# First keys through GpSimd in bf16, first queries through SyncE in fp32, and another order of the same work in an attention and mixer kernel

## The chip, the cores and the metric

The kernel runs on one core of one Trainium2 chip. The metric is the device time of one execution in microseconds; 352.54 us before, the median of three runs from 350.51 to 353.13. Every time below is in microseconds from the start of the profiled span if nothing else is said.

## The reference

Eight batches, twelve heads, sequence 448, head width 64. Attention with a squared ReLU in place of a softmax gives x (8 x 448 x 768); a token mixing and a channel mixing with two matrices each follow:

```
scores = (1/8) * q @ k.T
x      = (max(scores, 0)**2 / 448) @ v          # heads side by side: 768 columns
u      = x + (max(x.T @ w_tok1, 0) @ w_tok2).T  # 448 -> 256 -> 448
out    = u + max(u @ w_ch1, 0) @ w_ch2          # 768 -> 1536 -> 768
```

## The kernel before

**Tiling.** Four heads of one batch make a set; the 8 batches give 24 sets, numbered s. A set's keys, queries and values lie on 128 partitions in seven pieces c of 64 positions. `load` (L287) brings them in by GpSimd's queue, which turns fp32 into bf16 on the way: `ldk{s}`, `ldq{s}`, `ldv{s}`. For the sets 0 and 1 keys and queries come in halves of 64 partitions (`ldk1.0`, `ldk1.1`).

**One set.** `T{s}` transposes keys and queries on TensorE (line L404, 64x64 blocks), `cp` copies them from PSUM to the tile kqT; from set 12 on a copy (`ik`, `iq`) and a DMA transpose (`xk`, `xq`) on SyncE's queue take their place. `S{s}.{c}` is a score product (L442, four matmuls on the four 64x64 quarters of the array), `r{s}.{c}.{e}` its two evictions with the ReLU on ACT or DVE (L272, L274), `q{s}.{c}` the square on DVE (L449). `V{s}.{c}` is a value product (L466, also four 64x64 matmuls); the seven of a set accumulate in the same two PSUM banks, and `xe` evicts them. `X` and `xc` transpose x, `t1`, `rt`, `t2` and `u` are the token mixing.

**Channel mixing.** For the batches 0 and 1 `C1` computes the first product plainly; for the others `Q1` to `Q7` do it with seven products of blocks in place of eight (L629), with sums and differences (`m`, `y`), snapshots of a PSUM bank on ACT (`na`, `nb`, `nc`) and evictions on DVE (`h`). The second product does the same for pairs of 128 rows: `P1` to `P7` (L711), the sums `s1` to `s4`, the adds `a`, `b`, `c`, `f` on DVE (L727), the stores `st`.

**The order.** No scheduler orders the engines' work. The string `ORDER` (L62) names every operation once; `Order.run` (L43) emits them in its sequence, so each engine gets its instructions in the order of the words. `:A` or `:D` behind an eviction says ACT or DVE, digits behind a TensorE operation are its PSUM banks. `fill:7*24` stands for 24 filler matmuls into bank 7 (L811), which compute nothing that is used. Nine buffers hold squared scores, eight PSUM banks everything that TensorE writes.

**The start.** Eleven warm-up matmuls (L347) run on zeros. `load_first` (L353) brings set 0's first keys and queries as fp32, in halves of 64 partitions, half 1 ahead of half 0: the operation `ldf` issues the queries' half on SyncE's queue into a tile that the DMA transposes use later, and the keys' half on ScalarE's queue into two of the score buffers. Eight casts (`castk`, `castq`; two columns blocks e for each half) on ACT and DVE turn them into bf16. `ident` builds the identity on GpSimd, ahead of its first load. `T0.1` and `T0.0` transpose the two halves.

Of the kernel before, what the change touches and what calls it, by code (L numbers as in the profile page):

```python
# [62 lines left out]
ldf.1 ident ldf.0 ldk1.1 ldq1.1 ldk1.0 ldq1.0 castk0.1:A castk1.1:D castq0.1:D ldv0 castq1.1:A ldq2 T0.1:0  # L63
castk0.0:D castq1.0:A castk1.0:D castq0.0:A ldk2 cp0.1:D fill:1*6 T0.0:1 ldv1 cp0.0:A ldk3 fill:0*9 S0.2:23 ldq3
S0.3:45 S0.6:67 r0.2.0:D r0.2.1:A S0.4:01 wt1.1 r0.3.0:A r0.3.1:D S0.1:32 r0.4.1:A wt1.0 q0.2:D S0.0:45 r0.1.1:A
r0.1.0:D r0.0.0:A ldv2 T1.0:12 q0.3:D r0.0.1:A S0.5:34 ldq4 r0.4.0:A cp1.0:D r0.5.1:A q0.0:D ldk4 r0.5.0:A cp1.1:D
r0.6.1:A wt2 q0.1:D r0.6.0:A S1.1:50 S1.2:14 V0.0:32 q0.4:D r1.1.1:A V0.1 r1.1.0:A r1.2.0:D T2.0:76 r1.2.1:A q0.5:D
V0.2 S1.3:05 cp2.1:A V0.3 q0.6:D S1.0:14 q1.1:D r1.3.1:A r1.3.0:A cp2.0:D S1.6:65 V0.4 r1.0.1:A q1.2:D V0.5 r1.0.0:A
q1.3:D V0.6 r1.6.1:A S2.0:07 S1.4:41 ldv3 q1.0:D xe0.1:A r1.4.0:A r1.4.1:D ldk5 xe0.0:A r1.6.0:D ldq6 r2.0.0:A
q1.4:D X0.0:5 r2.0.1:A S1.5:24 ldq5 xc0.0:D S2.2:13 V1.0:60 r1.5.1:A r1.5.0:D V1.1 r2.2.1:A q1.6:D V1.2 r2.2.0:A  # L70
S2.1:75 q1.5:D V1.3 r2.1.1:A S2.5:42 V1.4 r2.1.0:D T3.0:31 r2.5.1:A q2.0:D r2.5.0:A V1.5 cp3.1:A V1.6 q2.1:D S2.3:57
S2.4:24 ldv4 cp3.0:D r2.4.1:A t1.0.0:1 r2.4.0:D ldk6 r2.3.1:A V2.0:34 q2.2:D r2.3.0:A wc1.0.2 V2.1 xe1.1:A q2.4:D
S3.1:27 X0.1:5 wc1.0.3 xe1.0:A q2.3:D V2.2 r3.1.1:A X1.1:0 wc1.0.0 q2.5:D r3.1.0:A fill:6*4 S2.6:67 xc1.1:D wc1.0.1
rt0.0:A V2.3 q3.1:D r2.6.0:A V2.4 wc1.1.1 S3.2:20 r2.6.1:A xc0.1:D V2.5 S3.0:16 r3.2.0:D r3.2.1:A wc1.1.3 T4.0:57
r3.0.0:A q2.6:D wc1.1.2 X1.0:0 r3.0.1:A cp4.0:D S3.4:21 xc1.0:A wc1.1.0 cp4.1:D r3.4.1:A t1.1.0:6 q3.0:D r3.4.0:A
V2.6 q3.2:D rt1.0:A S4.1:50 ldv5 xe2.1:A t2.0.0:7 q3.4:D xe2.0:A S3.3:12 u0.0:D X2.1:6 r4.1.1:A t1.0.1:4 r3.3.0:D
r3.3.1:A ldk7 S3.6:37 xc2.1:D rt0.1:A V3.0:01 r3.6.1:A q3.3:D t1.1.1:2 r3.6.0:A X2.0:4 r4.1.0:D ldq7 rt1.1:A S3.5:67
V3.1 q3.6:D xc2.0:A V3.2 r3.5.0:A r3.5.1:D S4.2:35 V3.3 S4.0:24 r4.2.1:A r4.2.0:D t2.0.1:6 ldq8 r4.0.0:A q3.5:D
T5.0:75 r4.0.1:A u0.1:D V3.4 S4.3:32 cp5.1:A V3.5 cp5.0:D ldk8 t2.1.1:4 q4.0:D r4.3.1:A V3.6 S5.1:67 r4.3.0:A u1.1:D
t1.2.0:5 xe3.1:A xe3.0:D ldv6 t1.2.1:2 rt2.0:A q4.3:D r5.1.0:A S5.0:34 X3.0:1 rt2.1:A q4.1:D r5.1.1:A S4.6:05 ldq9  # L80
xc3.0:D t2.2.0:6 r5.0.1:A t2.1.0:2 r4.6.1:A q4.2:D S4.4:71 r4.6.0:A u1.0:D t1.3.0:4 r4.4.1:A r4.4.0:D r5.0.0:A
u2.0:D V4.0:50 rt3.0:A S5.2:21 V4.1 q4.4:D S4.5:73 r5.2.0:A V4.2 r4.5.1:A q4.6:D V4.3 S5.3:64 r4.5.0:A r5.2.1:D
T6.0:23 r5.3.0:A q4.5:D V4.4 r5.3.1:A S5.6:71 ldk10 cp6.0:D t2.2.1:6 cp6.1:A C1.0.1a:4 q5.0:D ldq10 r5.6.1:A u2.1:D
wc2.00 S5.4:23 r5.6.0:A V4.5 q5.2:D S6.1:16 r5.4.1:A V4.6 r5.4.0:D t2.3.1:7 ldv7 xe4.0:A t2.3.0:3 q5.1:D xe4.1:A
# [24 lines left out]
C1.1.3:4 u7.0:D q11.0:D xd9 V10.2 m1.2:D c1e1.3:A S11.2:53 V10.3 S11.1:12 r11.2.0:A r11.2.1:D V10.4 S11.6:64
# [94 lines left out]
def kernel(ctx: ExitStack, tc: tile.TileContext, q: bass.AP, k: bass.AP, v: bass.AP, moe_w_tok1: bass.AP, moe_w_tok2: bass.AP, moe_w_ch1: bass.AP, moe_w_ch2: bass.AP, out: bass.AP):  # L204
# [637 lines left out]
```

## Time and profile before

| what | value |
|---|---|
| median of three runs | 352.54 us (350.51 to 353.13) |
| the profiled execution | 351.32 us |
| its span, first to last instruction | 349.6 us |
| mean granted TensorE clock | 0.995 |
| busy: TensorE, DVE, ACT, GpSimd | 337.4, 311.2, 222.3, 61.1 us |
| matmuls, of which fillers | 3910, 19 |
| moved by DMA | 48.99 MB |

In the profile PE is TensorE's matmuls and PEld its weight loads, DVE is VectorE, ACT ScalarE, POOL GpSimd, SP SyncE; a q behind a name is the engine's own queue of DMA issues and waits. A row of the timeline has its start, its length, the engine, the line, the tile written and the tile read, the shape of one instruction, their number, and in brackets the idle time before it with what ended it. A row of the stage table has the stretch, its length, the busy time of PE, PEld, DVE, ACT and POOL with the numbers of instructions, TensorE's granted clock, the DMA engines' busy share and the GB/s moved. Matmuls overlap, so what one costs is read from start to start.

### The profile page before, as it was taken

Reading aid. Unit: us, or ns where it says so; the run is one execution under the profiler, and the core shown is the slowest. Engines: PE = TensorE matmul, PEld = TensorE weight load, DVE = VectorE, ACT = ScalarE, POOL = GpSimd, SP = SyncE. Lnnn points to the kernel's source line nnn. Section 1 sums busy time; section 2 is a strip of 40 time slices with the busy share of each in tenths; the row PEclk is TensorE's granted clock in tenths of the full one; section 3 lists DMA queues with packets and bytes.
Section 4 is the critical chain, followed back from the end, with each engine's and each line's share of the span. In section 5 each row is a group of like instructions: output and inputs, shape, how many; then the busy total and the mean of one; then the engine's idle time right before and its main releaser. Section 6 shows DMA issues by size and latency. Waiting matters only on the chain.

```text
span 349.6 us, 9549 instructions
## 1 busy us (share of the span) xinstructions
PE 337.4 (97%) x3910; PEld 220.1 (63%) x3910; DVE 311.2 (89%) x597; ACT 222.3 (64%) x447; POOL 61.1 (17%) x93
## 2 busy tenths in 40 slices
PE   6778999999999999999999999999999999999994
PEld 2545555564455667766776576666776668887862
DVE  2799999999999998799999999999998976597693
ACT  3899998989895384298956669688645412321300
POOL 7536452303013210002114200000000000000000
PEclk9899999999999999999999999999999999999999
DMA  8999999999997996389999996798472507426517
GB/s 172 202 155 161 208 203 209 185 156 137 122 118 126 200 208 141 72 133 156 196 182 137 196 180 111 119 165 160 84 115 59 100 13 169 99 32 135 96 22 173
DMA packets 93276, 48.99 MB, mean 140 GB/s; under 512 B 67696, under 2 KB 89904, under 8 KB 93232
## 3 DMA queue, kind: packets, MB, share of 16 engines
q0 software_dynamic: 23088, 21.24, 40.8%
q1 hardware_dynamic: 68256, 26.29, 40.4%
q10 hardware_dynamic: 1888, 0.85, 1.1%
q8 instruction: 30, 0.49, 0.6%
q14 instruction: 14, 0.11, 0.1%
HBM read 43.38 MB, written 11.01 MB: 156 GB/s over the span
## 4 chain that ended last, share of the span: by engine, by line
PE 91%; ACT 4%; DMA 2%; issue 1%; DVE 0%; ACTq 0%
PE m_ps L711 28%; PE m_ps L629 21%; PE sc_ps L442 10%; PE acc_ps L466 10%; PE m_ps L556 8%; PE t_ps L510 6%; PE h_ps L519 6%; ACT sq L272 4%; DMA sq<-in_k_dram 2%; PE kqT_ps L404 1%; PE x_ps L501 1%; ACT kqT L278 0%; PE fill_ps L811 0%; DVE kq_raw L280 0%; ACT xT L476 0%
## 5 line engine op out<-in xcount | busy, mean ns | idle before, releaser
L272 ACT ACTIVATE sq<-sc_ps 128x448 bf16<-128x448 f32 x251 | 122.0, 579 | 15.8 <-PE sc_ps L442 15.3
L449 DVE TENSOR_TENSOR sq<-sq 128x896 bf16<-128x896 bf16 x168 | 98.1, 612 | 0.6 <-ACT sq L272 0.3
L442 PE MATMUL sc_ps<-kqT 64*64 64x448 bf16 x672 | 59.8, 360 | 1.9 <-DVE kqT L280 1.2
L278 ACT ACTIVATE snaps<-m_ps 128x448 f32<-128x448 f32 x50 | 27.8, 556 | 50.3 <-PE m_ps L629 23.9
L466 PE MATMUL acc_ps<-sq,v_raw 64*64 64x448 bf16 x672 | 57.1, 355 | 0.0
L274 DVE TENSOR_SCALAR sq<-sc_ps 128x448 bf16<-128x448 f32 x85 | 50.1, 613 | 5.2 <-PE sc_ps L442 5.1
L629 PEld LDWEIGHTS <-wc 128*128 128x128 bf16 x432 | 40.9, 98 | 7.4 <-issue 2.9
L711 PEld LDWEIGHTS <-r_sb 128*128 128x128 bf16 x336 | 32.4, 98 | 20.2 <-issue 1.6
L647 DVE CUSTOM_DVE_ANT_0 r_sb<-m_ps,snaps 128x448 bf16<-128x448 f32 x54 | 32.9, 616 | 8.5 <-PE m_ps L629 3.4
L272 ACT ACTIVATE r_sb<-m_ps 128x448 bf16<-128x448 f32 x41 | 22.7, 566 | 26.1 <-PE m_ps L629 17.2
L293 POOL DMA_DIRECT2D v_raw<-in_v_dram x24 | 17.2, 717 | 117.6 <-PE acc_ps L466 91.8
L727 DVE TENSOR_TENSOR out_sb<-m_ps,u_sb 128x384 f32<-128x384 f32 x56 | 30.7, 550 | 6.2 <-PE m_ps L711 6.1
L442 PEld LDWEIGHTS <-kqT 64*64 64x64 bf16 x672 | 23.2, 107 | 19.5 <-issue 10.0
L629 PEld LDWEIGHTS <-wy 128*128 128x128 bf16 x324 | 30.4, 98 | 6.4 <-issue 3.0
L711 PEld LDWEIGHTS <-sums 128*128 128x128 bf16 x252 | 24.1, 98 | 15.2 <-issue 1.8
L711 PE MATMUL m_ps<-wc_t,r_sb 128*128 128x384 bf16 x168 | 31.9, 326 | 0.0
L711 PE MATMUL m_ps<-wc,sums 128*128 128x384 bf16 x168 | 31.9, 326 | 0.0
L711 PE MATMUL m_ps<-wc,r_sb 128*128 128x384 bf16 x168 | 31.2, 326 | 0.0
L466 PEld LDWEIGHTS <-v_raw 64*64 64x64 bf16 x672 | 20.3, 105 | 17.0 <-issue 9.8
L556 PE MATMUL m_ps<-uT_sb,wc 128*128 128x448 bf16 x144 | 30.6, 353 | 0.0
L523 DVE TENSOR_TENSOR uT_sb<-h_ps,xT 128x448 bf16<-128x448 f32 x48 | 29.0, 612 | 1.4 <-PE h_ps L519 1.4
L727 DVE TENSOR_TENSOR out_sb<-m_ps,out_sb 128x384 f32<-128x384 f32 x42 | 22.9, 550 | 4.9 <-PE m_ps L711 4.8
(63 smaller groups left out, 436.1 us busy)
## 6 DMA issues: line engine op xcount, KB each, us to landing
out_dram<-out_sb SPq DMA_DIRECT2D x52, 192.0 KB, 3.0
v_raw<-in_v_dram POOLq DMA_DIRECT2D x24, 224.0 KB, 6.1
kq_raw<-in_q_dram POOLq DMA_DIRECT2D x22, 224.0 KB, 7.0
kq_raw<-in_k_dram POOLq DMA_DIRECT2D x22, 224.0 KB, 6.8
wc<-in_moe_w_ch_dram POOLq DMA_DIRECT2D x8, 288.0 KB, 11.0
wc<-in_moe_w_ch_dram POOLq DMA_DIRECT2D x4, 576.0 KB, 12.7
u_sb<-uT_sb SPq DMA_TRANSPOSE x48, 3.3
side<-in_q_dram SPq DMA_DIRECT2D x2, 224.0 KB, 5.6
```

The lines of the kernel that those rows point to most:

```text
L272: nc.scalar.activation(out, ps, AF.Relu)
L274: nc.vector.tensor_scalar(out=out, in0=ps, scalar1=0.0, scalar2=None, op0=ALU.max)
L278: nc.scalar.activation(out, ps, AF.Copy)
L442: nc.tensor.matmul(o.ps[e][64 * half:64 * (half + 1), :S], lhsT=lhsT, rhs=rhs, start=True, stop=True, skip_group_check=True)
L449: sq_ops[s, c] = [add(Op(f'q{s}.{c}', 'DVE', lambda o: nc.vector.tensor_tensor(out=buf, in0=buf, in1=buf, op=ALU.mult), ev))]
L466: nc.tensor.matmul(o.ps[half][64 * e:64 * (e + 1), :S], lhsT=r[rows, e, c * D:(c + 1) * D], rhs=sq[rows, e, :], start=c == 0, stop=c == KC ...
L523: nc.vector.tensor_tensor(out=uTs[bb % 2][:, 2 * i + a, off:off + S].rearrange('n (c p) -> n c p', c=KC), in0=t2.ps[:, :S].rearrange('n (p ...
L556: nc.tensor.matmul(ps[:, :S], lhsT=wc1[:, g, e * 128:(e + 1) * 128], rhs=uT[:, g, off:off + S], start=g == 0, stop=g == CC - 1)
L629: nc.tensor.matmul(banks[into][:, i * SH:(i + 1) * SH], lhsT=lhs[:, g, e * 128:(e + 1) * 128], rhs=rhs[:, g], start=after is None and i == ...
L647: nc.vector._custom_dve(TENSOR_ADD_SAT, out=out_, in0=ps, in1=snaps[z][:, :, x:y], s0=float('inf'), s1=0.0)
L711: nc.tensor.matmul(banks[into][:, :HN], lhsT=lhs[:, e], rhs=wc2[w][:, e], start=after is None and e == 0, stop=e == EH - 1, skip_group_che ...
L727: nc.vector.tensor_tensor(out=out_, in0=ps, in1=more, op=ALU.add)
```

## The change

Set 0's keys now come by the ordinary `load`, in two halves on GpSimd's queue and as bf16; the ScalarE DMAs, the fp32 place for the keys and the four key casts go. The queries still come as fp32 halves on SyncE's queue and are cast. `ORDER` is another one for all engines. Banks, the split of evictions between ACT and DVE, the sequence of loads on GpSimd, of transposes and stores on SyncE and of everything on TensorE differ almost throughout; the arithmetic is the same. Counted in the two strings: filler matmuls 19 and 78, in 3 and 9 places; value products that follow a value product 40 and 76; neighbours on TensorE of which one uses 64x64 quarters and the other the whole array 137 and 125; score evictions on DVE 85 and 75.

```diff
-    first = {'q': sides[0].rearrange('p a c d -> p (a c d)'), 'k': sq_all[:, NSQ - 2:].rearrange('p i a n -> p (i a n)')}
-    first = {t: x.bitcast(FP32).rearrange('p (e n) -> p e n', e=2) for t, x in first.items()}
+    q_first = sides[0].rearrange('p a c d -> p (a c d)').bitcast(FP32).rearrange('p (e n) -> p e n', e=2)
...
     def load_first():
+        rows = q[0].rearrange('h (p c) d -> (h p) (c d)', c=KC)[:256].rearrange('(e r) x -> r e x', e=2)
         for half in (1, 0):
             part = slice(64 * half, 64 * (half + 1))
 
             def emit(o, part=part):
-                for queue, src, dst in ((nc.sync, q, first['q']), (nc.scalar, k, first['k'])):
-                    rows = src[0].rearrange('h (p c) d -> (h p) (c d)', c=KC)[:256].rearrange('(e r) x -> r e x', e=2)
-                    queue.dma_start(out=dst[part], in_=rows[part])
-            ld = add(Op(f'ldf.{half}', 'SP', emit, whole=True))
-            for t in 'kq':
-                for e in range(2):
-                    o = Op(f'cast{t}{e}.{half}', ('DVE', 'ACT')[e], lambda o, t=t, e=e, part=part: copy(o, raws[t][0][part, e], first[t][part, e]), [ld])
-                    loads.setdefault((0, t), []).append(add(o))
+                nc.sync.dma_start(out=q_first[part], in_=rows[part])
+            ld = add(Op(f'ldf.{half}', 'SP', emit))
+            for e in range(2):
+                o = Op(f'castq{e}.{half}', ('DVE', 'ACT')[e], lambda o, e=e, part=part: copy(o, raws['q'][0][part, e], q_first[part, e]), [ld])
+                loads.setdefault((0, 'q'), []).append(add(o))
+        load(0, 'k')
     load_first()
```

Of the order string, its first lines:

```diff
-ldf.1 ident ldf.0 ldk1.1 ldq1.1 ldk1.0 ldq1.0 castk0.1:A castk1.1:D castq0.1:D ldv0 castq1.1:A ldq2 T0.1:0
-castk0.0:D castq1.0:A castk1.0:D castq0.0:A ldk2 cp0.1:D fill:1*6 T0.0:1 ldv1 cp0.0:A ldk3 fill:0*9 S0.2:23 ldq3
...
+ldf.1 ldk0.1 ldf.0 ldk0.0 ldq1.0 ldk1.0 ldk1.1 castq0.1:A castq1.1:D ldq1.1 ident castq0.0:D castq1.0:A ldv0 ldk2
+T0.1:0 T0.0:1 cp0.1:A ldq2 cp0.0:D ldv1 fill:2*7 S0.4:23 S0.5:45 ldq3 S0.3:67 r0.4.0:D r0.4.1:A S0.2:01 r0.3.0:A
...
+T1.0:56 r0.1.1:A r0.1.0:D ldk4 r0.5.0:A cp1.0:D cp1.1:A wt1.1 q0.0:D r0.6.1:A q0.1:D wt2 fill:7*24 S1.1:70 S1.4:14
```

Three places of the order, as the built programs have it. First GpSimd's queue at the program's start (kq_raw holds keys and queries, v_raw values, wt token weights). Before:

```order
L837 UNCONDITIONAL_BRANCH
masks.py:197 MEMSET ident 128x128
masks.py:199 ISA
masks.py:199 AFFINE_SELECT ident<-ident 128x128
L293 DMA kq_raw<-in_k_dram 64x2x448
L293 DMA kq_raw<-in_q_dram 64x2x448
L293 DMA kq_raw<-in_k_dram 64x2x448
L293 DMA kq_raw<-in_q_dram 64x2x448
L293 DMA v_raw_76<-in_v_dram 128x2x448
L293 DMA kq_raw<-in_q_dram 128x2x448
```

And after:

```order
L836 UNCONDITIONAL_BRANCH
L293 DMA kq_raw<-in_k_dram 64x2x448 x2
L293 DMA kq_raw<-in_q_dram 64x2x448
L293 DMA kq_raw<-in_k_dram 64x2x448 x2
L293 DMA kq_raw<-in_q_dram 64x2x448
masks.py:197 MEMSET ident 128x128
masks.py:199 ISA
masks.py:199 AFFINE_SELECT ident<-ident 128x128
L293 DMA v_raw_76<-in_v_dram 128x2x448
L293 DMA kq_raw<-in_k_dram 128x2x448
```

Two issues for set 0's keys came to the head, the identity moved behind six issues, and v0 stands behind all of them.

Second, DVE from its first cast on (side is the tile with the fp32 queries, sq the score buffers, whose last two held the fp32 keys). Before:

```order
L280 CAST kq_raw<-sq 64x448
L280 CAST kq_raw<-side_82 64x448
L280 CAST kq_raw<-sq 64x448 x2
L280 COPY kqT_79<-kqT_ps 128x896
L274 TENSOR_SCALAR sq<-sc_ps 128x448 x2
L449 TENSOR_TENSOR sq<-sq 128x896
```

And after:

```order
L280 CAST kq_raw<-side_82 64x448 x2
L280 COPY kqT_79<-kqT_ps 128x896
L274 TENSOR_SCALAR sq<-sc_ps 128x448 x3
L448 TENSOR_TENSOR sq<-sq 128x896 x2
L274 TENSOR_SCALAR sq<-sc_ps 128x448
```

The casts of keys are gone; the copy that DVE makes was that of half 1 and is that of half 0, the last one that the first score product waits for.

Third, TensorE at the last value product, V23.6 (acc_ps is written by value products, m1_ps by the first channel product, m2_ps by the second). Before:

```order
L629 MATMUL m1_ps_5188<-mt_85,wc1_69 128x224
L466 LDWEIGHTS v_raw2_78
L466 MATMUL acc_ps_5039<-sq_83,v_raw2_78 64x448
L466 LDWEIGHTS v_raw2_78
L466 MATMUL acc_ps_5039<-sq_83,v_raw2_78 64x448
L466 LDWEIGHTS v_raw2_78
L466 MATMUL acc_ps_5040<-sq_83,v_raw2_78 64x448
L466 LDWEIGHTS v_raw2_78
L466 MATMUL acc_ps_5040<-sq_83,v_raw2_78 64x448
L711 LDWEIGHTS sums_74
```

And after:

```order
L465 MATMUL acc_ps_5308<-sq_83,v_raw2_78 64x448
L465 LDWEIGHTS v_raw2_78
L465 MATMUL acc_ps_5307<-sq_83,v_raw2_78 64x448
L465 LDWEIGHTS v_raw2_78
L465 MATMUL acc_ps_5307<-sq_83,v_raw2_78 64x448
L465 LDWEIGHTS v_raw2_78
L465 MATMUL acc_ps_5308<-sq_83,v_raw2_78 64x448
L465 LDWEIGHTS v_raw2_78
L465 MATMUL acc_ps_5308<-sq_83,v_raw2_78 64x448
L628 LDWEIGHTS wy_84
```

It stood alone between two channel products, a change of form on each side; now it follows V23.5, and shares those changes with it.

More of the change, by code (lines that the diff above doesn't have):

```diff
@@ L68 @@
[L68 to L72, printed above, removed]
@@ new lines @@
+Q6.2.1 a.2:D Q3.2.0 P6.2 h12.2.0:D nb.2.1:A t1.10.0:2 b.2:D Q4.2.0 rt10.0:A Q7.2.1 h21.2.0:A t2.10.1:5 nc.2.1:A
+Q6.2.2 u10.1:D t2.9.1:4 h22.2.1:D P7.2 u9.1:D Q3.2.1 c.2:D S12.3:20 h12.2.1:D S12.6:54 r12.3.1:A Q4.2.1 xq15
+r12.6.1:D r12.6.0:A P5.2:6 nb.2.2:D r12.3.0:A h21.2.1:A q12.6:D st2.1 Q5.2.2:0 q12.3:D ub2.1 Q7.2.2 f22.2:D
+t2.10.0:4 nc.2.2:A P3.2 xk15 u10.0:D h22.2.2:D P4.2 iq16:A m1.3:D ub2.3 f12.2:D Q3.2.2 f21.2:D Q4.2.2 h12.2.2:D
+V12.0:52 h21.2.2:A S13.2:34 V12.1 S13.3:67 r13.2.0:A r13.2.1:D V12.2 S13.4:01 r13.3.1:A r13.3.0:D V12.3 V12.4
@@ new lines @@
+Q4.7.0 h21.7.1:A st22.0 Q7.7.2 h21.7.0:A st22.1 P4.11 nc.7.2:A h22.7.2:D Q4.7.2 f21.11:D P1.12:2 h21.7.2:A st23.1
+s1.12:D P2.12:6 st23.0 a.12:D s2.12:D Q3.7.2 s3.12:D P5.12:4 s4.12:D h12.7.2:D P6.12 f11.12:D s1.13:D P1.13:5 b.12:D
+s2.13:D P2.13:1 s3.13:D a.13:D P7.12 f11.13:D st26.1.0 P6.13 c.12:D st26.0.0 f22.12:D P4.12 b.13:D P3.12 f21.12:D
+st25.0 P7.13 s4.13:D st25.1 f12.12:D P5.13:0 c.13:D st24.0 st24.1 P4.13 f22.13:D st27.1.384 P3.13 f21.13:D
+st27.0.384 st27.0.0 f12.13:D st27.1.0 st26.1.384 st26.0.384
```

255 lines of the change are left out of this document (125 added, 130 removed).

## The prediction

> **What bounds the kernel now.** I read the page first (busy shares and slices), then the stage table, then the start in the table by microsecond, the chain and the timeline, and last the channel stage's timeline. From the page:
>
> ```profile
> span 349.6 us, 9549 instructions
> PE 337.4 (97%) x3910; PEld 220.1 (63%) x3910; DVE 311.2 (89%) x597; ACT 222.3 (64%) x447; POOL 61.1 (17%) x93
> PEclk9899999999999999999999999999999999999999
> ```
>
> The span is 349.6 us; the profiled execution took 351.32, so 1.7 lies around it, and it is 1.2 below the median 352.54 (runs from 350.51 to 353.13). TensorE is busy for 97%, and its clock is below full in one slice of 40, the second. Three stages (columns: length, then PE, PEld, DVE, ACT and POOL busy with their counts, clock, DMA share, GB/s):
>
> ```profile
> 13.00:35.00 22.00, 17.45 (x441) 10.18 (x437) 22.00 (x43) 22.00 (x50) 10.58 (x17) 1.00 1.13 167
> 35.00:45.00 10.00, 10.00 (x181) 5.73 (x178) 10.00 (x20) 10.00 (x24) 4.86 (x7) 1.00 1.17 207
> 45.00:330.00 285.00, 284.89 (x3095) 189.37 (x3094) 262.49 (x500) 183.70 (x366) 35.54 (x51) 1.00 0.81 136
> ```
>
> From 45 to 330 TensorE has 0.11 us without work: there only fewer or cheaper matmuls help, or shorter gaps between them. From 13 to 35 the bound is the eviction: DVE and ACT have 22.00 of 22.00, TensorE waits 4.55. Ahead of that lies the start:
>
> ```profile
> 7.00:8.00 1.00, 0.00 (x0) 0.00 (x0) 0.00 (x0) 0.00 (x0) 0.00 (x0) 1.00 1.25 199
> 8.00:9.00 1.00, 0.21 (x1) 0.10 (x1) 0.93 (x3) 0.67 (x2) 0.94 (x2) 1.00 1.28 205
> 9.00:10.00 1.00, 0.98 (x28) 0.92 (x29) 0.49 (x1) 0.37 (x1) 1.00 (x2) 0.51 1.25 201
> 11.00:12.00 1.00, 1.00 (x13) 0.55 (x16) 0.35 (x1) 0.31 (x1) 0.45 (x1) 0.50 1.26 202
> 12.00:13.00 1.00, 1.00 (x16) 0.64 (x9) 1.00 (x3) 0.97 (x3) 0.71 (x1) 0.79 1.26 202
> ```
>
> From 7 to 8 no engine works and the DMA engines are full at some 200 GB/s; from 9 to 12.4 the clock is half. The chain says for what everything waits (start, length), and the timeline shows the steps behind it:
>
> ```profile
> 1.49 6.56 DMA sq<-in_k_dram
> ```
>
> ```profile
> 0.74 1.64 SPq L360 DMA_DIRECT2D side<-in_q_dram  x2
> 1.44 0.73 POOL L293 DMA_DIRECT2D kq_raw<-in_k_dram  x1
> 3.33 0.62 POOL L293 DMA_DIRECT2D kq_raw<-in_q_dram  x1
> 3.91 0.76 POOL L293 DMA_DIRECT2D v_raw<-in_v_dram  x1
> 5.83 0.63 PE L404 MATMUL kqT_ps<-ident,kq_raw 64*64 64x64 bf16 x28
> 6.39 0.51 PE L811 MATMUL fill_ps<-out_sb 128*128 128x128 bf16 x6
> 8.33 1.04 ACT L278 ACTIVATE kq_raw<-side 64x448 bf16<-64x448 f32 x2 [2.49 <-DMA side<-in_q_dram]
> 8.51 0.21 PE L404 MATMUL kqT_ps<-ident,kq_raw 64*64 64x64 bf16 x1 [1.61 <-DVE kq_raw L280]
> 8.89 0.60 DVE L280 COPY kqT<-kqT_ps 128x896 bf16<-128x896 bf16 x1
> 9.02 0.99 PE L404 MATMUL kqT_ps<-ident,kq_raw 64*64 64x64 bf16 x27 [0.30 <-DVE kq_raw L280]
> 9.94 1.14 PE L811 MATMUL fill_ps<-out_sb 128*128 128x128 bf16 x9
> 10.05 0.92 ACT L278 ACTIVATE kqT<-kqT_ps 128x896 bf16<-128x896 bf16 x1 [0.68 <-PE kqT_ps L404]
> 11.02 1.33 PE L442 MATMUL sc_ps<-kqT 64*64 64x448 bf16 x12
> 16.36 0.72 PE L466 MATMUL acc_ps<-sq,v_raw 64*64 64x448 bf16 x8
> ```
>
> The second half of the fp32 keys lands at 8.05, the second half of the queries at about 8.3; casts, transposes at half clock (0.99, where the first half took 0.63 at full clock) and ACT's copy (0.92) follow, and the first score product starts at 11.02.
>
> **Part 1, the first loads (the main term).** The two ACT issues (224 KB each, fp32) and four casts go; two POOL issues of 112 KB come, at the head of POOL's queue, with q1 and k1 behind them and the building of the identity behind all six. Transfer times known here (KB each, median us from issue to landing; then min/median/max of POOL's loads into kq_raw up to 14 us):
>
> ```profile
> kq_raw<-in_k_dram POOLq DMA_DIRECT2D x2, 112.0 KB, 6.2
> side<-in_q_dram SPq DMA_DIRECT2D x2, 224.0 KB, 5.6
> sq<-in_k_dram ACTq DMA_DIRECT2D x2, 224.0 KB, 5.1
> DMA to landing us min/median/max: 6.0/6.8/8.0
> ```
>
> POOL begins at 0.74 (where the identity started), issues every 0.62 to 0.73, so the second key half is issued at 1.47, and the identity is ready at about 0.74 + 0.73 + 5 x 0.62 + 0.65 = 5.2, before the transposes need it. If POOL's loads keep their 6.0 to 8.0, it lands at 7.5 to 9.5. But those times were measured under 4 x 224 + 4 x 112 = 1344 KB, which at some 210 GB/s from 2.0 us on last until 8.4: that is when the old halves landed. Now what must move is at least 2 x 224 + 2 x 112 = 672 KB (until 5.2), at most also the four halves of q1 and k1, 1120 KB (until 7.3). I take 6.8, nearer the upper end, because the old halves landed only when about everything issued had moved. Then: query cast 0.57, transposes at full clock 0.63, copy now on DVE 0.60, hand-offs 0.2: first score at 8.8 for 11.02, a gain of 2.2. Bounds: keys at 9.5 and half clock (0.99) give 11.3, a loss of 0.3; keys at 5.2 give 7.2, a gain of 3.8. Since DVE and ACT are then full until 45, and the work per score is unchanged, an earlier first score moves everything by as much, as long as the loads keep up: 224 KB less are moved, 1.1 us of the queue at 210 GB/s. POOL's two extra issues (1.35 us) delay v0 and k2 in its queue; the old v0 issue stood at 3.91, and the first value product came at 16.36, 5.3 us behind the first score, which hides it.
>
> The Trainium skill, "DMA: Bandwidth & Descriptors" (Latency and other measured facts), speaks against this step: about 1 us to the first byte for a DMA that GpSimd issues, about 0.6 for one issued by SyncE or ScalarE. As an estimate from that page the gain would be 0.4 less, 1.8 in place of 2.2; the rows above lean the same way, 6.2 for the smaller GpSimd load and 5.1 for ACT's.
>
> **Part 2, filler matmuls.** The order holds 78 filler matmuls in place of 19, 59 more. At full clock one takes about 0.057 (0.51 us for six, less the 0.22 of the last one's drain), so 59 cost 3.4 us if TensorE had other work, nothing if they stand where it waits. All 78 stand ahead of V3.0 in the order table, in the stretch where TensorE waits 4.55 + 1.6. I take 0; bounds 0 and +3.4. At half clock (9.94, nine in 1.14, one every 0.107) they cost twice as much: this is the slow rival.
>
> About the clock: TensorE stood idle for 1.61 us, and worked for about 1.5 of the 3.4 us before 9.0; the 3.4 us after that ran at half. The Trainium skill, "TensorE: Matmul & The Clock Gate" (Why this matters for your kernels), asks only that no idle gap exceed about 3 us, by which before would have kept its clock. The trace disagrees: 1.6 us were enough. By the page the changed kernel would keep full clock too, and the sum stays; by the rows a half clock is possible, and the first score comes 0.4 later.
>
> **Part 3, changes of matmul form.** Score and value products use 64x64 quarters of the array, channel products the whole. In the channel stage:
>
> ```profile
> 240.50 0.78 PE L466 MATMUL acc_ps<-sq,v_raw 64*64 64x448 bf16 x12
> 241.06 0.58 PE L442 MATMUL sc_ps<-kqT 64*64 64x448 bf16 x4
> ...
> 242.64 0.75 PE L629 MATMUL m_ps<-mt,wy 128*128 128x224 bf16 x6
> 243.23 0.74 PE L629 MATMUL m_ps<-uT_sb,wc 128*128 128x224 bf16 x6
> 243.89 0.38 PE L442 MATMUL sc_ps<-kqT 64*64 64x448 bf16 x4
> 244.11 0.36 PE L466 MATMUL acc_ps<-sq,v_raw 64*64 64x448 bf16 x4
> 244.30 0.36 PE L442 MATMUL sc_ps<-kqT 64*64 64x448 bf16 x4
> 244.59 0.75 PE L629 MATMUL m_ps<-uT_sb,wy 128*128 128x224 bf16 x6
> ```
>
> Start to start: a channel product followed by its like takes 0.59, followed by a score 0.66; a score followed by a value 0.22 or 0.19, by a channel product 0.29. A change of form costs 0.07 to 0.10, say 0.09. Counting the order table, before has 137 such changes, after 125; behind V4.0, which falls into the stage without idle time, 103 and 97. There 6 x 0.09 = 0.55 are saved; the other six lie where TensorE waits anyway and count 0.
>
> **Part 4, value products in a row.** Three in a row take 241.06 - 240.50 = 0.56, so 0.19 each, as between scores. Neighbours of this kind rise from 40 to 76. They cost the same either way, so by themselves they bring 0; they are what lowers the changes of form.
>
> **Part 5, moved evictions.** By the order table ten score evictions go from DVE (85 to 75) to ACT (251 to 261), five token evictions the other way. In the long stage DVE has 22 us to spare and ACT 101, TensorE none: 0. New waits of the new order I bound by +-1 for 285 us: in the rows one score takes 0.22 and the few that wait some tenth more. The tail (last products, adds and stores) is the same but for queue names: 0.
>
> **Sum.** -2.2 - 0.55 + 0 + 0 + 0 = -2.75: 351.32 becomes 348.6 on the profiled execution's footing, 349.8 on the median's. I give 348.9, nearer the profile since its rows carry the sum.
>
> **The rivals.**
> A, the gain is hidden: the first halves wait for DMA bandwidth as before, since POOL's six halves run beside the queries (share 1.25 and more). Keys land at 8 or later, the first score comes 0 to 1 earlier, and with part 3 the time is about 351.0. For it: no POOL load landed in under 6.0. Against: half of the key bytes are gone. Chance 0.22.
> B, slower: fillers on the path. If the clock is still half when the 24 fillers between T1.0 and S1.1 come, they last 24 x 0.107 = 2.6 where the copies they cover take about 1.5 (0.92 on ACT, behind an eviction of about DVE's 0.60); and if the waits for which the other 35 new fillers stand are shorter than planned, those add up to 35 x 0.057 = 2.0. It decides against the change from 2.75 us of uncovered fillers on: with all 59 in the way, partly cold, 3.4 + 1.2, it gives 351.3 - 2.75 + 4.6 = 353.2. For it: half clock at this very place in before. Against: full clock follows after one such stretch. Chance 0.14.
> C, more: the keys land at 5.5, the clock stays full, and the wait of 4.55 shrinks by 1.5 beyond the shift: -3.6 - 0.55 - 1.5, about 345.7. Chance 0.13.
> The forecast itself has 0.51, with a range of its own from 347.4 to 350.3.
>
> **How the numbers follow.** A measurement of this kernel can tell about 1%, 3.5 us, from no change: faster means below 349.0. The forecast's own range is halved by that line: 0.27 faster, 0.24 same; C goes to faster, A to same, B to same for 0.05 and to slower (above 356.1, which takes fillers at half clock throughout) for 0.09. So faster 0.40, same 0.51, slower 0.09. The range takes in A and half of C and B: 346.3 to 352.3.
>
> **What would show it.** First score product between 8.4 and 9.4; key halves landing before 7.5; the idle 7-to-8 row filled; clock 1.00 or one half stretch; DVE and ACT still full from the first score to 45; fillers followed by a wait, not by a late score; scores to channel products 0.29 still. The prediction is wrong if POOL's first loads need their old 6 to 8 us, if TensorE's first 35 us hold more than one slow stretch, or if the stretch from 45 to 330 has new gaps.

## The result, and the profile after

The changed kernel took 354.52 us, the median of 20 runs (351.47 to 359.19); the kernel before took 351.67 beside it, also 20 runs (350.51 to 354.9). The ratio, of mean times without the two runs of the changed kernel that count as slow (356.85 and 359.19), is 1.0059, with a 95% interval from 1.0032 to 1.0087: slower by 0.6%, less than the 1% named in the prediction. The medians' quotient is 1.0081. The profiled execution took 355.84, 1.3 above that median, so the parts read from it below add up to a little more than the medians show.

The page of the changed kernel:

```profile
span 354.1 us, 9659 instructions
PE 339.4 (96%) x3969; PEld 222.6 (63%) x3969; DVE 306.7 (87%) x585; ACT 225.5 (64%) x455; POOL 62.4 (18%) x95
PEclk9999999999999999999999879999999999999999
```

The second slice of the clock row, which was the only weak one before, is full. Two slices in the middle, from about 195 to 212 us, are weak instead. The stage table says the same (columns as before: stretch, length, PE, PEld, DVE, ACT and POOL busy, clock, DMA share, GB/s):

```profile
7.00:8.00 1.00, 0.78 (x15) 0.53 (x19) 0.62 (x1) 0.60 (x1) 1.00 (x2) 1.00 1.29 190
9.00:10.00 1.00, 1.00 (x12) 0.42 (x7) 1.00 (x3) 1.00 (x4) 1.00 (x3) 1.00 0.97 132
35.00:45.00 10.00, 9.34 (x182) 5.55 (x174) 8.85 (x17) 8.92 (x21) 2.40 (x4) 1.00 1.20 206
45.00:195.00 150.00, 149.95 (x1816) 93.41 (x1815) 142.66 (x268) 116.84 (x235) 33.95 (x48) 1.00 1.03 153
195.00:207.50 12.50, 6.73 (x27) 3.37 (x26) 6.32 (x13) 3.12 (x6) 0.00 (x0) 0.73 1.38 200
207.50:330.00 122.50, 122.50 (x1197) 88.41 (x1196) 105.27 (x202) 63.93 (x129) 2.82 (x4) 1.00 0.54 102
```

The row from 7 to 8 is filled, and 9 to 10 runs at full clock. From 45 to 195 and from 207.5 to 330 TensorE has next to no idle time. Nearly all the loss sits in 12.5 us between: 12.50 - 6.73 = 5.77 us without work, and a mean clock of 0.73, which is 2 x 0.27 x 12.5 = 6.75 us at half speed (the clock record in the trace has it from 200.61 to 207.44, 6.83 us). In the same stretch the kernel before had no idle time and full clock:

```profile
195.00:207.50 12.50, 12.50 (x101) 7.99 (x100) 12.50 (x27) 6.97 (x16) 2.12 (x3) 1.00 1.28 198
```

To see where time was gained and lost, I gave every product on TensorE except the fillers its usual time, added these up in each trace, and compared when the same sum of work was reached. The table has the difference to the kernel before in us (negative is earlier). 25 us of work are done at about 48 us of the span, 100 at 128, 160 at 192, 200 at 234. The experiments' columns are used further on.

```
work done   changed   spread   loads only   few fillers   best
      1.5     -3.5     -3.4       -2.6         -2.8       -3.1
       25     -1.7     -1.6       -1.9         -2.5       -2.9
      100     -3.0     -3.0       -2.0         -3.8       -4.2
      160     -3.4     -2.3       -1.9         -3.7       -3.6
      170     +5.3     -0.1       -1.9         +0.9       -1.3
      200     +5.0     +0.1       -0.8         +0.6       -1.0
      300     +4.4     -0.4       -0.8         -0.1       -1.4
```

The changed kernel is 3.4 us ahead at 160 us of work, loses 8.7 within the next ten, and takes 0.9 back until the end.

**The start.** The timeline of the changed kernel:

```profile
1.25 1.33 POOL L293 DMA_DIRECT2D kq_raw<-in_k_dram  x2 [0.80 <-POOLq L825]
5.79 0.60 DVE L280 CAST kq_raw<-side 64x448 bf16<-64x448 f32 x1 [1.12 <-DMA side<-in_q_dram]
6.00 0.99 PE L403 MATMUL kqT_ps<-ident,kq_raw 64*64 64x64 bf16 x56
7.71 2.55 PE L441 MATMUL sc_ps<-kqT 64*64 64x448 bf16 x28 [0.23 <-DVE kqT L280]
```

The second query half is there at 5.79 (its cast begins), the second key half landed at 6.30, both sets of transposes take 0.99 together at full clock, and the first score product starts at 7.71 where it started at 11.02.

**The stall.** The chain of waits through it (start, length), and the rows of TensorE, ACT and DVE behind it, each in its own timeline:

```profile
191.16 0.26 ACT sq L272
191.42 8.89 DMA kqT<-side
...
200.40 0.16 ACT side L278
...
201.25 0.54 ACT sq L272
...
201.83 1.65 PE h_ps L518 x4
```

```profile
195.32 0.74 PE L628 MATMUL m_ps<-uT_sb,wc 128*128 128x224 bf16 x6
201.83 1.65 PE L518 MATMUL h_ps<-wt,r_sb 128*128 128x448 bf16 x4 [5.77 <-ACT sq L272]
203.27 2.13 PE L710 MATMUL m_ps<-wc_t,sums 128*128 128x384 bf16 x6
```

```profile
191.02 1.01 ACT L272 ACTIVATE sq<-sc_ps 128x448 bf16<-128x448 f32 x2
200.40 0.95 ACT L278 ACTIVATE side<-kq_raw 128x896 bf16<-128x896 bf16 x1 [8.36 <-DMA kqT<-side]
201.25 1.83 ACT L272 ACTIVATE sq<-sc_ps 128x448 bf16<-128x448 f32 x4
```

```profile
202.24 0.63 DVE L448 TENSOR_TENSOR sq<-sq 128x896 bf16<-128x896 bf16 x1 [4.84 <-ACT sq L272]
```

The row of ACT at 200.40 is `iq20`, the copy of set 20's queries into the tile side. There is one such tile, so `iq20` must wait until `xq19`, the DMA transpose of the set before, has read it. That transpose was issued at 191.42 and landed at 200.31. ACT takes its instructions in order, so four evictions of scores and a snapshot stood behind `iq20`, which waited for 8.36 us, though TensorE had written the scores by 193.8. TensorE ran on for some 4 us with what it had, then had no more; when it could go on, six channel products took 2.13 in place of 1.14. A chain view calls this "DMA", but the DMA was late by its own slowness, and what made it slow is in the row of POOL:

```profile
190.14 1.41 POOL L293 DMA_DIRECT2D v_raw<-in_v_dram  x2 [15.96 <-PE acc_ps L465]
191.53 0.72 POOL L293 DMA_DIRECT2D kq_raw<-in_q_dram  x1
192.23 2.14 POOL L293 DMA_DIRECT2D kq_raw<-in_k_dram  x3
```

GpSimd stood for 15.96 us at the load `ldv19`, which needs a buffer that the value product V16.6 frees. Five other loads stood behind it in the same queue, `ldv18`, `ldq23`, `ldk20`, `ldk21` and `ldk23`, whose buffers had been free since between 151 and 186 us. At 190.14 all six, 224 KB each, went out in 4.2 us, and `xq19` was issued into the middle of them. The DMA issues of the stretch from 190 to 200 and of the quiet one from 208 to 240 (number, KB, median us from issue to landing):

```profile
kq_raw<-in_k_dram POOLq DMA_DIRECT2D x3, 224.0 KB, 11.6
...
u_sb<-uT_sb SPq DMA_TRANSPOSE x2, 9.5
kqT<-side SPq DMA_TRANSPOSE x2, 9.7
```

```profile
kqT<-side SPq DMA_TRANSPOSE x6, 3.0
u_sb<-uT_sb SPq DMA_TRANSPOSE x5, 3.1
```

A transpose takes 3.0 us when little else moves and 9.7 beside the burst. The Trainium skill, "DMA: Bandwidth & Descriptors" (Issuing engines are not separate DMA queues), says that DMAs started by different engines run on the same 16 DMA engines and interleave. The rows agree: SyncE's transposes stretch by GpSimd's loads.

The slow transfer is one part of the wait; the other is that `xq19` was issued late. The copy that it reads, `iq19`, was done at 183.99, and 7.4 us went by until 191.42, in which SyncE's queue issued in its order four transposes of u, one of x and a store. ACT's row, and the first of SyncE's:

```profile
183.03 0.96 ACT L278 ACTIVATE side<-kq_raw 128x896 bf16<-128x896 bf16 x1
```

```profile
183.35 4.64 SPq L534 DMA_TRANSPOSE u_sb<-uT_sb  x3
```

As an estimate from these rows, the same 8.89 us from 184 on would have ended at about 192.9, less than 1 us after ACT came to `iq20` at 192.04. No run tried this.

Before, transposes were slow at the same place too:

```profile
kqT<-side SPq DMA_TRANSPOSE x2, 6.7
```

```profile
207.42 1.00 ACT L278 ACTIVATE side<-kq_raw 128x896 bf16<-128x896 bf16 x1
```

There `iq20` started at 207.42 without waiting, since it stood 81 words of the order behind `xq19`; `xq19` had landed at 200.51. In the changed order it stands 44 words behind.

Nor are bursts new. Before, GpSimd waited 11.75 us for a buffer and then issued five loads in 3.5 us, ahead of this very `xq19`, which was issued at 193.35 and took 7.2:

```profile
187.73 0.70 POOL L293 DMA_DIRECT2D kq_raw<-in_q_dram  x1 [11.75 <-ACT side L278]
...
190.51 0.73 POOL L293 DMA_DIRECT2D v_raw<-in_v_dram  x1
```

And the changed kernel has an earlier burst of five, from 170.66 to 174.2, beside which `xq18` and `xk18` took 8.8 and 8.2 (the second row, from 170 to 184). TensorE lost nothing there: `xq18` had landed at 182.47, before ACT came to `iq19` at 183.03.

```profile
170.66 0.71 POOL L293 DMA_DIRECT2D kq_raw<-in_q_dram  x1 [5.53 <-ACT side L278]
```

```profile
kqT<-side SPq DMA_TRANSPOSE x2, 8.5
```

So a burst alone need not cost time; it does where an instruction that others stand behind needs the slow transfer soon.

### The profile page after: what moved, and what is told of

It reads as the page before. It is cut to its first block, busy times and chain, and to the rows that moved or that the text cites. A ratio compares the mean times of both kernels' runs of the same rounds, so it can differ in the third digit from the quotient of the medians.

```text
span 354.1 us, 9659 instructions
## 1 busy us (share of the span) xinstructions
PE 339.4 (96%) x3969; PEld 222.6 (63%) x3969; DVE 306.7 (87%) x585; ACT 225.5 (64%) x455; POOL 62.4 (18%) x95
## 4 chain that ended last, share of the span: by engine, by line
PE 87%; ACT 6%; DMA 4%; issue 1%; DVE 0%; ACTq 0%
PE m_ps L710 26%; PE m_ps L628 20%; PE sc_ps L441 9%; PE acc_ps L465 8%; PE m_ps L555 8%; PE t_ps L509 6%; PE h_ps L518 6%; DMA kqT<-side 4%; ACT sq L272 4%; PE warm_ps L348 1%; PE kqT_ps L403 1%; PE x_ps L500 1%; ACT kqT L278 1%; PE fill_ps L810 0%; ACT xT L475 0%
## 5 line engine op out<-in xcount | busy, mean ns | idle before, releaser
L272 ACT ACTIVATE sq<-sc_ps 128x448 bf16<-128x448 f32 x261 | 127.5, 594 | 25.5 <-PE sc_ps L441 22.6
L278 ACT ACTIVATE snaps<-m_ps 128x448 f32<-128x448 f32 x52 | 28.9, 561 | 50.9 <-PE m_ps L628 32.7
L441 PE MATMUL sc_ps<-kqT 64*64 64x448 bf16 x672 | 57.7, 356 | 1.8 <-DVE kqT L280 1.2
L465 PE MATMUL acc_ps<-sq,v_raw 64*64 64x448 bf16 x672 | 49.0, 352 | 0.0
L274 DVE TENSOR_SCALAR sq<-sc_ps 128x448 bf16<-128x448 f32 x75 | 44.9, 619 | 2.9 <-PE sc_ps L441 2.9
L441 PEld LDWEIGHTS <-kqT 64*64 64x64 bf16 x672 | 20.4, 105 | 20.7 <-issue 12.1
L710 PE MATMUL m_ps<-wc,sums 128*128 128x384 bf16 x168 | 32.9, 333 | 0.0
L278 ACT ACTIVATE side<-kq_raw 128x896 bf16<-128x896 bf16 x24 | 24.3, 1012 | 11.1 <-DMA kqT<-side 11.1
L518 PE MATMUL h_ps<-wt,r_sb 128*128 128x448 bf16 x96 | 25.4, 362 | 5.8 <-ACT sq L272 5.8
L293 POOL DMA_DIRECT2D kq_raw<-in_k_dram x26 | 18.3, 707 | 66.7 <-ACT side L278 60.7
## 6 DMA issues: line engine op xcount, KB each, us to landing
wc<-in_moe_w_ch_dram POOLq DMA_DIRECT2D x4, 576.0 KB, 11.3
```

What stands on the lines that cost most here:

```text
L272: nc.scalar.activation(out, ps, AF.Relu)
L274: nc.vector.tensor_scalar(out=out, in0=ps, scalar1=0.0, scalar2=None, op0=ALU.max)
L278: nc.scalar.activation(out, ps, AF.Copy)
L293: nc.gpsimd.dma_start(out=raws[t][s % NR[t]][part], in_=rows[part])
L441: nc.tensor.matmul(o.ps[e][64 * half:64 * (half + 1), :S], lhsT=lhsT, rhs=rhs, start=True, stop=True, skip_group_check=True)
L465: nc.tensor.matmul(o.ps[half][64 * e:64 * (e + 1), :S], lhsT=r[rows, e, c * D:(c + 1) * D], rhs=sq[rows, e, :], start=c == 0, stop=c == KC ...
```

## The experiments

So there were two theories. One: the burst is the cause; loads held up behind one that can't go yet come out together, and stretch every transpose, whoever waits for it. The other: the place of `iq20` is the cause; transposes are slow there in any case, and the new order has a copy too early in ACT's queue. A third, that SyncE's queue issues `xq19` late (theory Q in the texts below), was named but has no experiment of its own. Two more questions were what the new first loads are worth by themselves, and whether the 78 fillers cost anything. The kernels below are edits of the order string, shown as its words; the one with the new first loads alone takes the changed `load_first` besides; line numbers of their profiles are a few lower.

**The burst spread.** The five loads are moved to where their buffers come free; nothing else changes.

```diff
   q13.6:D ik16:A
+  ldk20
...
   st4.1 ik17:A
+  ldk21
...
   ub3.5 V15.6
+  ldv18
...
   Q7.3.2 iq19:A
+  ldq23
...
   P4.4 ik19:A
+  ldk23
...
   h22.3.2:D xe16.0:A
-  ldv18
   xk19 r18.1.1:A s2.5:D t1.14.0:6
-  ldq23
   r18.1.0:A s3.5:D iq20:A f11.4:D
-  ldk20
   P1.5:3 rt14.0:D
-  ldk21
   m1.4:D S18.0:20 S17.3:57
-  ldk23
```

Expected:

> The changed kernel with five load words moved ahead in the order table (k20 behind the copy ik16, k21 behind ik17, v18 behind V15.6, q23 behind iq19, k23 behind ik19), so that they are issued when their buffers come free and not in one burst behind v19. Theory L (six loads issued within 4 us at 190 fill the DMA engines, the transposes xq19, xk19 and xq20 take 9 to 10 us, and ACT, which has iq20 next in its queue, waits for xq19): xq19 lands in 3 to 4 us, the 5.8 us gap of TensorE at 196 and the half clock behind it go, 8 us less than the changed kernel, 345 to 347, ratio to before 0.982 to 0.988. Theory Q (xq19 is issued late by SyncE's own queue, the loads only add): the gap shrinks to 2 to 3 us, 348 to 350. Theory O (the stall comes of other evictions of the new order): unchanged, 354.

Measured: 351.1 us (349.88 to 353.69), ratio 0.9987, interval 0.9955 to 1.002; the profiled execution has a span of 349.4 and full clock in every slice. Its GpSimd, ACT, TensorE and DMA rows (the last from 190 to 200):

```profile
187.09 0.70 POOL L291 DMA_DIRECT2D kq_raw<-in_k_dram  x1 [1.00 <-ACT side L276]
191.25 0.70 POOL L291 DMA_DIRECT2D v_raw<-in_v_dram  x1 [3.46 <-PE acc_ps L463]
```

```profile
197.34 0.95 ACT L276 ACTIVATE side<-kq_raw 128x896 bf16<-128x896 bf16 x1 [4.21 <-DMA kqT<-side]
```

```profile
198.78 0.97 PE L516 MATMUL h_ps<-wt,r_sb 128*128 128x448 bf16 x4 [1.61 <-ACT sq L270]
```

```profile
kqT<-side SPq DMA_TRANSPOSE x2, 4.3
```

With one load where six were, the transposes there take 4.3 in the median for 9.7 (`xq19` itself 5.05 for 8.89), ACT's wait is halved, TensorE's gap is 1.61 for 5.77, and the clock stays full in the profile. The burst cost the changed kernel 2.5 us by the two ratios (1.0059 against 0.9987) or 3.4 by the medians (354.52 against 351.1); the two intervals lie apart. The time stays above the 345 to 347 and the 348 to 350 that two of the theories gave. Not everything is gone: the copy still waits 4.21 (`xq19` was issued 7.1 us after `iq19` here too, at 192.21 after 185.09), and another, `iq16`, waits 2.99 for `xq15` (2.71 in the changed kernel); by work 160 this profile is 1.1 us less ahead than that of the changed kernel.

**The copy moved, the burst kept.** `iq20` and its transpose go to just ahead of `ik20`.

```diff
   r18.1.0:A s3.5:D
-  iq20:A
   f11.4:D ldk20
...
   r17.6.0:A Q6.4.0
-  xq20
   s2.6:D r17.1.1:A
...
   Q2.4.0:5 q17.3:D
+  iq20:A xq20
   ik20:A f21.5:D
```

Expected:

> The changed kernel with the copy iq20 and its transpose xq20 moved behind, to just ahead of ik20; the burst of loads stays. Theory L with ACT's queue as the link: xq19 still takes 8 to 10 us, but ACT goes on with the score evictions, so that TensorE's gap falls below 1 us and the clock stays full: 345 to 347. If the burst alone is to blame whatever stands in ACT's queue (another consumer of a slow transfer stalls next, the set 19's scores or a store's tile): a gap of 2 to 6 us moves some us later, 350 to 354. Theory O: unchanged, 354.

Measured: 355.72 us (353.03 to 357.16, four runs), ratio 1.0102, interval 1.0049 to 1.0156; span 354.3. The rows of ACT, TensorE and of the DMA issues from 190 to 200:

```profile
206.39 0.95 ACT L276 ACTIVATE side<-kq_raw 128x896 bf16<-128x896 bf16 x1
210.54 0.95 ACT L276 ACTIVATE side<-kq_raw 128x896 bf16<-128x896 bf16 x1 [3.20 <-DMA kqT<-side]
```

```profile
212.41 1.28 PE L626 MATMUL m_ps<-mt,wc 128*128 128x224 bf16 x6 [3.33 <-ACT snaps L276]
```

```profile
kqT<-side SPq DMA_TRANSPOSE x2, 10.4
```

`iq20` no longer waits. But `xk19`, issued at 198.63, landed at 210.44, and now `ik20` waits for that one; a snapshot stands behind it on ACT, and TensorE waits for the snapshot. The stall moved by some 11 us (201.83 to 212.41), and the time didn't fall: 350 to 354 had been expected for this outcome, 345 to 347 for the other. So with this burst moving one copy only chose another instruction to pay; the second theory alone falls.

**The new first loads alone.** The order of before, with its first words replaced:

```diff
   ldf.1
+  ldk0.1 ldf.0 ldk0.0 ldq1.0 ldk1.0 ldk1.1 castq0.1:A castq1.1:D ldq1.1
   ident
-  ldf.0 ldk1.1 ldq1.1 ldk1.0 ldq1.0 castk0.1:A castk1.1:D castq0.1:D
+  castq0.0:D castq1.0:A
   ldv0
-  castq1.1:A
   ldq2 T0.1:0
-  castk0.0:D castq1.0:A castk1.0:D castq0.0:A
```

Expected:

> The kernel before with the new first loads alone: keys of set 0 by GpSimd in halves, identity behind six issues, key casts gone; the rest of its order word for word, with its 19 fillers. Theory of the prediction (an earlier first score moves everything, since DVE and ACT are the bound until 45): first score at 8 to 9.2 in place of 11.0, and 1.8 to 2.5 us less at the end, 349 to 350, ratio 0.993 to 0.995. Theory H (what is gained at the start is lost again before 35, since the later loads or the evictions hold the rest): first score earlier, the end within 0.7 us of before.

Measured: 350.75 us (349.42 to 353.03), ratio 0.9976, interval 0.9948 to 1.0003. By the table the first scores come 2.6 us earlier, 1.9 are left from work 25 to 170 without any change, and 1.1 of them is lost around one new wait:

```profile
228.53 0.38 PE L438 MATMUL sc_ps<-kqT 64*64 64x448 bf16 x3 [0.67 <-ACT r_sb L269]
```

The loads are worth about 1.9 us up to there and 0.8 to 1.2 in the time. The second is the difference of the medians, 351.92 beside it; the interval just reaches 1, and 350.75 is above the 349 to 350 that the prediction's theory gave.

**Few fillers.** The spread kernel, with only `fill:2*7` and `fill:5*4` of the nine groups of fillers left; the 67 that go compute nothing that is used.

```diff
-  fill:7*24
...
-  fill:0*4
...
-  fill:3*3
...
-  fill:0*3
...
-  fill:5*9
...
-  fill:3*15
...
-  fill:1*9
```

Expected:

> The first of these kernels (loads spread) with 11 fillers in place of 78: only the seven ahead of the first score and the four ahead of T1.0 stay; 67 are gone. If fillers stand where TensorE waits (the prediction) and serve only the clock: without them half the clock comes back in one or two stretches between 9 and 26, which the evictions mostly hide: 0 to 1.5 us more than with them. If they are on the path (the slow rival): up to 3 us less than with them. If they do neither: the same within 0.5.

Measured: 352.3 us (350.74 to 356.13), ratio 1.0005, interval 0.9982 to 1.0029. The stretch from 4 to 35, and that of the stall:

```profile
4.00:35.00 31.00, 25.27 (x554) 14.83 (x552) 27.56 (x53) 27.99 (x60) 20.54 (x32) 1.00 1.21 189
...
195.00:207.50 12.50, 9.81 (x62) 5.55 (x60) 9.91 (x21) 5.28 (x11) 0.00 (x0) 0.86 0.74 166
```

The clock is full from 4 to 35 without them, and by the table this kernel is 0.8 us further ahead at work 25 and 100 than the spread one (-2.5 and -3.8 against -1.6 and -3.0). So in this profile the fillers weren't needed for the clock there, and cost about 0.8 of their 67 x 0.057 = 3.8. The size is loose: the late copy and the kernel with both edits have the same order as the spread one up to there, all 78 fillers, and by the same count -0.2 and -1.0 at work 25. The two profiles with eleven fillers, -2.5 and -2.9, lie ahead of all four with 78. The time didn't follow: in its profile `iq20` waited 5.28 for `xq19`, TensorE stopped for 2.69 and then ran for about 3.5 us at half clock (2 x 0.14 x 12.5; the clock record has 3.41, from 198.87 to 202.28). Against the spread kernel the medians (352.3 and 351.1) are no evidence for a gain; 0 to 1.5 more had been expected of a clock lost between 9 and 26, and that isn't where this profile lost it.

**Spread, and the copy late.** Both edits of the first two experiments together; of the diff against the changed kernel, the part around `iq20`.

```diff
   r18.1.0:A s3.5:D
-  iq20:A
   f11.4:D P1.5:3
...
   Q2.4.0:5 q17.3:D
+  iq20:A xq20
   ik20:A f21.5:D
```

Expected:

> The changed kernel with both edits: the five loads spread, and the copy iq20 with its transpose xq20 behind, just ahead of ik20. Theory L in two links (the loads stretch the transposes; ACT's queue passes the wait on): the 1.78 us gap that the spread alone left at 196, where ACT still waited 4.2 us for xq19, goes, with the half us or so behind it: 2 to 3 us less than the spread alone, 348 to 349.5, ratio to before 0.989 to 0.993. Theory Q (SyncE's queue issues xq19 and xk19 late, whatever the rest): ik20 then waits for xk19 instead, and the gap moves to 205 to 210 with 1 to 3 us: no better than the spread alone, 351.

Measured: 351.74 us (349.29 to 353.07), ratio 0.9995, interval 0.9965 to 1.0025: no better than the spread alone, where 348 to 349.5 had been expected if the late copy helped. The wait on `iq20` is gone, but in the profile, which is of the longest of its twelve runs (353.07), ACT and DVE have others:

```profile
147.44 0.95 ACT L276 ACTIVATE side<-kq_raw 128x896 bf16<-128x896 bf16 x1 [4.47 <-DMA kqT<-side]
167.26 0.95 ACT L276 ACTIVATE side<-kq_raw 128x896 bf16<-128x896 bf16 x1 [2.52 <-DMA kqT<-side]
```

```profile
199.40 0.56 DVE L724 TENSOR_TENSOR out_sb<-m_ps,u_sb 128x384 f32<-128x384 f32 x1 [2.43 <-DMA u_sb<-uT_sb]
```

Behind the first, `iq16` for `xq15`, TensorE waits 1.80; behind the add on DVE, which waits for a transpose of u, 1.48.

**Best guess.** Spread loads (with `ldk20` behind `ik17` and `ldk21` behind `ldk22`, so that fewer meet `xq15` and `xq16`), the copies `iq20` and `iq16` and their transposes late, and eleven fillers. In part, against the spread kernel:

```diff
   h22.2.2:D P4.2
-  iq16:A
...
   r13.5.1:A P2.2:1
-  xq16
...
   Q2.2.2:4 q13.6:D
+  iq16:A xq16
   ik16:A
...
   st4.1 ik17:A
-  ldk21
+  ldk20
...
   P3.3 ldk22
+  ldk21
...
   Q2.4.0:5 q17.3:D
+  iq20:A xq20
   ik20:A f21.5:D
```

Expected:

> The changed kernel with the loads spread a little otherwise (k20 behind ik17, k21 behind k22, v18, q23 and k23 as before), the copies iq20 and iq16 with their transposes moved to just ahead of ik20 and ik16, and 11 fillers in place of 78. If fillers cost 0.8 us on the path (what the few-fillers run showed at 100 us) and the wait of iq16 for xq15 costs 0.3 to 1.6 at 146: 1 to 2 us less than the kernel with both edits, 346.5 to 348.5, ratio 0.984 to 0.99. If the few-fillers run's lead was chance: the same as the kernel with both edits.

Measured: 350.0 us (348.5 to 352.19), ratio 0.9943, interval 0.9914 to 0.9971: faster than the kernel before by 0.6%, and by about 1.2% faster than the changed one (0.9943 / 1.0059, from two comparisons with the kernel before). It misses the 346.5 to 348.5 expected, though it is 1.7 below the kernel with both edits, inside the 1 to 2 expected. Several words were moved at once, so which of them brought it isn't shown. Full clock in every slice; the longest wait left on TensorE in the middle:

```profile
201.64 1.14 PE L707 MATMUL m_ps<-wc_t,r_sb 128*128 128x384 bf16 x6 [1.51 <-DVE out_sb L723]
```

**The order of before, with the copy early.** `iq20` 43 words behind `xq19` (44 in the changed order), and for its sake `ldq20` earlier.

```diff
   t2.12.0:5 ldq22
+  ldq20
   xk18 r15.6.1:D
   u14.0:D xd16
-  ldq20
...
   q17.2:D r17.0.0:A
+  iq20:A
   ub4.5 r18.1.0:A
...
   q17.3:D Q7.4.0
-  iq20:A
   q17.1:D P3.5
```

Expected:

> The kernel before with one copy moved: iq20 stands 44 words behind xq19 in the order, as in the changed kernel, in place of 81, and its load q20 behind q22, so that it is there in time. Everything else, the old first loads too, is as before. Theory L: in before xq19 took 7.2 us from 193.35 on without harm; now ACT waits for it from about 197 until 200.5, and TensorE loses 1 to 4 us near 200: 353 to 356, ratio 1.003 to 1.011. Theory Q or O (the place of the copy alone does nothing; it needs the changed kernel's other order): within 0.5 us of before.

Measured: 353.94 us (352.41 to 360.11), ratio 1.007, interval 1.0042 to 1.0098. The size is in the range expected of the early copy, 353 to 356, but its profile, which is of its shortest execution, 352.41, doesn't show it there. The rows of ACT:

```profile
187.54 0.95 ACT L276 ACTIVATE side<-kq_raw 128x896 bf16<-128x896 bf16 x1 [2.05 <-DMA kqT<-side]
...
201.58 0.96 ACT L276 ACTIVATE side<-kq_raw 128x896 bf16<-128x896 bf16 x1
```

`iq20` starts at 201.58, as soon as `xq19` has landed (201.50), and TensorE loses next to nothing at that place; the wait that shows, 0.93 on TensorE at 188.97, is behind `iq19` at 187.54, which waited for `xq18`. That transpose took 5.57 for 4.31 before, from 181.89 on, while the last two of a group of four loads issued from 173.7 to 176.5 were still landing (until 182.72 and 183.87); the moved `ldq20` is the last of them. So it shows that two words moved near a burst cost 0.7%, and not by which of the two; that the range was met is luck as far as this profile goes.

## Why the prediction was wrong

**What bounds the kernel** was read rightly: from 45 to 195 TensorE has 0.05 us without work after, 0.10 before, and there only its own products count. It did not hold for the new order's 12.5 us behind that.

**Part 1, the first loads** (-2.2, first score at 8.8). The mechanism was right and larger at its place: the second keys landed at 6.30 for 6.8, the clock was full, the first score came at 7.71, 3.3 earlier. The step "an earlier first score moves everything by as much" failed in part: by work 25 only 1.7 of 3.5 were left, with the old order 1.9 of 2.6. From 35 to 45 DVE and ACT were to be full and had 8.85 and 8.92 of 10, and TensorE waited 0.66 there, so that not the evictions alone set the pace. Rival A, the hidden gain, is excluded by the landing. The Trainium skill, "DMA: Bandwidth & Descriptors" (Latency and other measured facts), has a later first byte for a DMA that GpSimd issues; no run tells it apart in the 3.54 and 4.33 us in which 112 KB issued at 1.25 and 1.97 landed, at 4.79 and 6.30. One sum of this part is uneven: the bound of 11.3 leaves out the cast of 0.57 that the two others have, with which it is 11.9. Half clock at the start, which the prediction feared, matters little there: the last experiment's profile has 6.83 us of it (8.07 to 14.89) where before has 3.41, and by the same count the two are level at work 25.

**Part 2, the fillers** (0, bounds 0 and +3.4). They cost about 0.8 on the path, by the pair of profiles with and without 67 of them. Rival B, which had them at half clock, did not come: the clock was full up to the stall. The time ended on its side for another reason. Rival C, the larger gain, was near at first (3.4 us ahead at work 160, where it asked for 5.65 in all) and went with the stall.

**Part 3, form changes** (-0.55). Between work 25 and 160 the changed kernel gained 1.6 more, the old order with the new loads 0.0, with TensorE busy throughout in both. So the new order does make TensorE's own stream cheaper, by about three times the term, which was sized too small. Whether all of it is changes of form wasn't tried. **Part 4** (0 by itself) can't be told apart from it.

**Part 5** is the step that failed: "New waits of the new order I bound by +-1 for 285 us." The new wait was one of 5.77 us, with 6.75 us at half clock behind it, 8.7 in all between work 160 and 170. The bound came from small waits of rows of the old order; it holds only while no buffer's chain changes. The working set side by side what each engine executes, and did not ask, for each wait in the queues of GpSimd and ACT, what stands behind it. In the order string both facts could be read: five loads behind `ldv19`, and `iq20` 44 words behind `xq19` with one tile between them. The trace of before had its own warning, the five loads let go at 187.73 after a wait of 11.75. Only the durations, 9 us for a transpose beside six loads, were in no row of that stretch; the nearest was 7.2 for `xq19` before.

**The sum.** On the profiled executions: 351.32 - 1.7 (to work 25) - 1.6 (to 160) + 8.7 (to 170) - 0.95 (to the end) = 355.8, for 355.84 measured; these are differences of the same two traces, so they must add up. Taking the 8.7 out leaves 347.1, which would be within 2 us of the working's 348.6. No run shows that: the spread kernel's profiled execution took 351.20, since 2.2 of its lead went between work 160 and 170 all the same, and its ratio of 0.9987 is no change. So even without the burst the forecast gain of 2.75 isn't reached.

**What stays open.** Why the first 25 us of work keep only part of the earlier start. What makes the transposes differ from run to run: the spread kernel and the one with few fillers differ in nothing near 190 us, and `xq19` held ACT up for 4.21 and 5.28. What an earlier place of `xq19` in SyncE's queue would bring. The share of the early copy alone in the last experiment. And the stall was seen in one profile of the changed kernel; that it is in most runs is argued from the clock, 0.990 or less in twelve of the 20 runs, which took 353.25 to 359.19, while the other eight took 351.47 to 354.9. That argument is weak: of the kernel before, 14 of the 25 runs beside the first experiments show 0.990 or less too, at 351.44 to 354.13.

## What to carry to other kernels

When an order of instructions is changed, walk each in-order queue and ask at every instruction that can wait what stands behind it: a load that must wait for a buffer, put ahead of loads that need not, saves them up and lets them go at once. A burst is paid by an instruction that needs one of the stretched transfers soon and has others behind it. Here moving that instruction only changed who paid, and spreading the loads to where their buffers come free took most of it away. Ask of the transfer, too, how long it stood in its own queue before it was issued. An engine that is idle by four fifths, as GpSimd is here, can still set the time.

## What the runs showed of the hardware

A DMA transpose of 128 x 896 bf16 on SyncE's queue took 3.0 us with little beside it, 4.3 beside one load of 224 KB and stores, 6.7 (before) and 8.5 (changed, near 174) beside or just behind five such loads, and 9.7 to 10.4 beside six.

The clock: 5.77 us without a matmul brought half clock for 6.83 us by the trace's clock record (changed kernel), 3.33 and 2.69 brought 3.41 each (late copy, few fillers), and gaps of 1.61 (spread) and 1.80 (spread and late) none. At the start of the old order a gap of the same 1.61 was followed by 3.41 us of half clock (9.01 to 12.42), and one of 1.31 in the last experiment by 6.83 (8.07 to 14.89). So the length of the gap alone doesn't decide. The Trainium skill, "TensorE: Matmul & The Clock Gate" (What's actually happening), describes a window of about 3.4 us that runs freely and isn't set off by the kernel; stretches of half clock of 3.41 and 6.83 us, one and two such windows, and one gap with two outcomes agree with that; what ends or begins a window no run here shows.
